# Table scatters of a group made independent, and a second buffer for gathered rows

## The chip, the cores and the metric

The kernel runs on one core of a Trainium2 chip. The metric is device time in microseconds (us) of one execution, taken as the median of three. The engines are named as in the profile: PE (TensorE, matmuls; PEld its weight loads), DVE (VectorE), ACT (ScalarE), POOL (GpSimd) and SP (SyncE, which here only issues DMAs). Each engine runs its own instructions in a fixed order and waits on semaphores for the others and for DMAs.

## The reference

Three layers in a row, in float32. First a chunked attention: 4 batches, 8 heads, 768 positions, chunks of 32 with 16 positions of context to the left, 8 to the right and 8 memory positions. Its output is a matrix of 3072 tokens by 512. Then a dense gated layer, and then a routed layer in which each token goes to one of 8 experts:

```python
g = x @ w_gate;  silu = g * (1.0 / (1.0 + np.exp(-g)));  val = x @ w_val
x = silu * val @ w_out                       # 512 -> 1536 -> 512

logits = x @ w_gate;  e_idx = np.argmax(logits, axis=1)
gate_w = softmax(logits)[np.arange(N), e_idx]
eom = 1.0 / (1.0 + np.exp(-(x @ w_output_gate)))
for e in range(8):
    mask = e_idx == e
    h = np.maximum(x[mask] @ w1[e], 0.0)     # 512 -> 1024
    out[mask] = gate_w[mask, None] * eom[mask, e, None] * (h @ w2[e])
```

## The kernel before

**Groups.** The first two layers run in 8 groups of 384 tokens (`NG`, `GT`). A group's dense layer is 12 chunks `f` of 128 hidden columns: `m1_gate` and `m1_val` (L484, a product of split parts, three matmuls each) and `m1_out` (L525). The weights of each chunk are split anew into a high part, which ACT casts, and a low part, which POOL subtracts (L176, L177: `gvh` and `gvl` for gate and value, `oh` and `ol` for the output). PE needs `gvl` of chunk f + 1 from the third matmul of that chunk on. The attention pieces of the next group are spread between these chunks.

**The table.** When a group is done (`m1_done`), each of its tokens gets an expert and a place in that expert's list. Three scatters (`rt_R`, L668, 128 tokens each, an indirect DMA that POOL issues) write the tokens' numbers into `table` in DRAM, and one DMA of SP writes the tokens' rows into `xs` (L654). `later(delay, ...)` puts such pieces off by a number of ticks; there are three ticks to a chunk `f` in the groups and two to a chunk in the routed layer. The framework makes each scatter wait for the one before it to land, since both write `table`.

**Steps.** The routed layer runs in steps: steps 0, 1 and 2 hold the first 256 tokens of experts 0, 1 and 2 from groups 0 to 6 (`NEARLY` = 3, the early experts), the others are laid out by a schedule that DVE works out from the counts (`make_schedule`). A step has 8 chunks `n` (`NFE`). For a step, SP loads the token numbers out of the table (`load_idx`, tile `idx`, L844), POOL gathers the rows by them (`gather`, tile `xg`, L853, one indirect DMA for 128 rows), `prep_x` transposes them on PE (L871) and splits them. For a chunk, `split_chunk` (L826, L828) makes a high part on ACT and the low part in two halves, one on DVE (for `mm1`) and one on POOL (for `mm2`), under the names `wh`, `wl`, `gvh`, `gvl` in turn. `mm1` (L884) and `mm2` (L906) multiply, and `evac_y` and `scatter_y` (L922, on POOL) send the results out. `mm2` of a chunk stands behind `mm1` of the next.

**The order around the change.** In the last group the `idx` of steps 0 to 2 are loaded at chunk 7, `gather(0)` stands at the end of chunk 8 and `gather(1)` at the end of chunk 11. `xg` has one buffer, so `gather(2)` stands in the first chunk of step 1, behind the transposes of the rows of step 1, and step 2's rows are transposed from the fifth chunk of step 1 on:

```python
if j == 0 and (s >= NEARLY or 0 < s < NEARLY - 1):
    gather(s + 1)
    if s >= NEARLY:
        load_idx(s + 2)
```

The last group's scatters run in step 1 as well; at chunk `ready` = 14 SP loads `idx` of steps 3 and 4, and behind them in SP's queue stand the weight loads of the scheduled steps.

Of the kernel before, what the change touches and what calls it, by code (L numbers as in the profile page):

```python
# [21 lines left out]
def tile_chunk_attention_moe_moe2(  # L22
# [511 lines left out]
    def later(delay, fn, *args):  # L534
        nonlocal serial
        serial += 1
        todo.append((clock + delay, serial, fn, args))
        todo.sort(key=lambda x: x[:2])
# [86 lines left out]
    def rt_2(st, g):  # L625
        ps = ps_a.tile([P, GJ + 1, E], F32, tag="a", name="ps_r")
        for j in range(GJ + 1):
            for i in range(min(j + 1, GJ)):
                nc.tensor.matmul(
                    ps[:, j, :], tri if i == j else ones, st["ohb"][:, i, :],  # L630
                    start=(i == 0), stop=(i == min(j, GJ - 1)))
        r = small("r")
        tt(r, ps[:, 0:GJ, :], base.to_broadcast([P, GJ, E]), ALU.add)
        tt(base, ps[:, GJ:GJ + 1, :], base, ALU.add)
        tt(r, r, st["oh"], ALU.mult)
        pos = small("pos", (P, GJ, 1))
        red(pos, r, ALU.add)
        posi = small("posi", (P, GJ, 1), I32)
        nc.vector.tensor_copy(posi, pos)
        for j in range(GJ):  # L640
            later(1 + (3 if g < NG - 1 else 2) * j, rt_R, posi, g, j)
        if g == NG - 2:
            tt(base, base, mbase, ALU.max)

# [14 lines left out]
    def independent(inst, n, reason):  # L659
# [3 lines left out]
            tc.declare_no_dep(inst.ins, prev.ins, reason=reason)  # L663
        scattered.append(inst)

    def rt_R(posi, g, j):
        tk = g * GJ + j
        nc.gpsimd.indirect_dma_start(  # L668
            out=table, out_offset=bass.IndirectOffsetOnAxis(ap=posi[:, j, :], axis=0),
            in_=tokid[:, tk:tk + 1], in_offset=None)  # L670


    def ts(out_, a, s1, op0, s2=None, op1=None):
# [9 lines left out]
    def make_schedule():  # L683
# [83 lines left out]
        "ra": ("rwa", NRA, [P, 2, KD * P], F32), "w": (wrp, NF, [P, 2, KD * P], F32),  # L767
        "wh": ("p", 2, [P, 2, KD * P], F32R), "wl": ("p", 2, [P, 2, KD * P], F32R),
        "gvh": (jp, 2, [P, 2, KD * P], F32R), "gvl": (jp, 2, [P, 2, KD * P], F32R),
        "idx": (sm, 4, [P, 3], I32), "xg": ("p", 1, [P, 3, XW], F32),  # L770
        "xh": (xp, 2, [P, KD, 2 * P], F32R), "xl": (xp, 2, [P, KD, 2 * P], F32R),
        "sc": (sm, 3, [P, 3, 1], F32), "a": (ps_a, 3, [P, KD, P], F32),
        "g": (ps_g, 2, [P, 2 * P], F32), "o": (ps_o, GJ, [P, DM], F32),
# [58 lines left out]
    def load_idx(s):  # L832
        if s >= NSTEP:
            return
        e, nt = steps[s]
        idx = m2_tile(s, "idx")
        if e is not None:
            src = table[e * ES:e * ES + nt * P, :]
        else:
            d = s - NEARLY  # L840
            rv = nc.sync.value_load(
                sched_i[0:1, 1, d:d + 1], min_val=0, max_val=NTAB - nt * P)
            src = table[bass.ds(rv, nt * P), :]
        nc.sync.dma_start(out=idx[:, 0:nt], in_=src.rearrange("(t p) o -> p (t o)", p=P))  # L844
        idxs[s] = idx

    def gather(s):
# [80 lines left out]
    with tc.manual_schedule():  # L928
# [16 lines left out]
        for g in range(NG):  # L945
# [22 lines left out]
            for f in range(NF):  # L968
# [26 lines left out]
                if g == NG - 1:  # L995
                    if NRA + f < NEARLY * NFE:
                        load_chunk(NRA + f)
                    if f == 7:
                        for s in range(NEARLY):
                            load_idx(s)  # L1000
                    if f == 8:
                        gather(0)
                    if f in (10, 11):
                        prep_x(0, f - 10)
                    if f == 11:
                        gather(1)
                    if f >= 10:
                        split_chunk(f - 10)
        m1_out(NG - 1, NF - 1)
# [17 lines left out]
        def run_step(s, cond):  # L1027
            nonlocal nextc, pend
            for j in range(NFE):
# [19 lines left out]
                pend = (n, h)  # L1049
                if not cond and s + 1 < NUNC and 4 <= j < 7:  # L1050
                    prep_x(s + 1, j - 4)
                if j == 0 and (s >= NEARLY or 0 < s < NEARLY - 1):
                    gather(s + 1)
                    if s >= NEARLY:
                        load_idx(s + 2)
                tick()

        def finish():
# [51 lines left out]
```

## Time and profile before

| | us |
|---|---|
| median of 3 runs | 1177.03 (1175.99 to 1178.24) |
| the profiled execution | 1184.21 |
| span of its instructions | 1182.5 |
| PE busy | 1134.3 (96%) |
| POOL busy | 670.4 (57%) |
| ACT busy | 610.7 (52%) |
| DVE busy | 586.3 (50%) |

A row of a timeline is one instruction, or several alike in a row: start and duration in us, engine, line, operation, the tile written and the tiles read, and in brackets how long the engine had been idle before it and what ended that. The duration of an indirect DMA on POOL is the time in which POOL issues it, not the time until the data have landed. The attention takes the first part of the span, groups 0 to 7 follow one another until about 813 us, and the routed layer ends the program.

### The profile page before, as it was taken

To read this page: it belongs to the slowest core of one execution; us is meant where nothing else is said; L and a number is where in the kernel's file an instruction comes from. 1 tells how busy PE (TensorE), PEld (TensorE's weight loads), DVE (VectorE), ACT (ScalarE), POOL (GpSimd) and SP (SyncE) were. 2 spreads that over 40 slices of the span, in tenths; PEclk is the share of its full clock that TensorE was granted. 3 is DMA by queue.
4 is the path that set the end of the run, shared out by engine and by line. 5 is a ranking of instruction groups with operands and counts; after the bars stand their busy time and mean duration, and the time that the engine had idled before them with its cause. 6 is when DMAs were issued, how large, how long until landed. Compare 5 with 4: busy or idle time off the path is not lost.

```text
span 1182.5 us, 19838 instructions
## 1 busy us (share of the span) xinstructions
PE 1134.3 (96%) x7173; PEld 1019.6 (86%) x7173; DVE 586.3 (50%) x1162; ACT 610.7 (52%) x1318; POOL 670.4 (57%) x459
## 2 busy tenths in 40 slices
PE   7898999999999999999999999989889999999994
PEld 6787899998998998989899899878779899999994
DVE  6699845444444533544543433434854443444541
ACT  4688855555554545555555544434434443344551
POOL 4589844544644654454455465565476555656773
PEclk6799999999999999999999999999989999999998
DMA  8776524111211211211210100344369445555673
GB/s 206 193 216 206 147 78 117 36 35 43 48 30 28 64 35 35 55 43 24 63 37 14 42 7 19 92 96 160 51 186 342 150 146 161 174 162 190 208 221 119
DMA packets 204957, 126.52 MB, mean 107 GB/s; under 512 B 110960, under 2 KB 181744, under 8 KB 204850
## 3 DMA queue, kind: packets, MB, share of 16 engines
q1 hardware_dynamic: 199282, 110.70, 33.5%
q0 software_dynamic: 5568, 14.45, 4.1%
q8 instruction: 59, 0.97, 0.4%
q14 instruction: 48, 0.39, 0.1%
HBM read 111.61 MB, written 14.82 MB: 107 GB/s over the span
## 4 chain that ended last, share of the span: by engine, by line
PE 56%; issue 18%; POOL 8%; DVE 8%; DMA 4%; ACT 4%; SPq 1%; POOLq 0%; ACTq 0%; DVEq 0%
PE ps_g L484 28%; PE acc L525 14%; PE ps_att L350 3%; PE g L884 2%; POOL wl L828 2%; PE ps_pv L402 2%; PE o L906 2%; PE ps_t L322 2%; POOL out_dram L922 2%; POOL gvl L828 1%; PE ps_att L385 1%; PE ps_x L570 1%; DMA xg<-xs,idx 1%; DVE ps_c L225 1%; DVE w L228 1%
## 5 line engine op out<-in xcount | busy, mean ns | idle before, releaser
L177 POOL TENSOR_TENSOR gvl<-w,gvh 128x1024 fp32r<-128x1024 f32 x96 | 231.4, 2411 | 96.2 <-ACT gvh L176 95.3
L484 PE MATMUL ps_g<-xh,gvh 128*128 128x384 f32 x768 | 272.3, 355 | 0.6 <-ACT gvh L176 0.6
L484 PE MATMUL ps_g<-xh,gvl 128*128 128x384 f32 x768 | 262.8, 342 | 6.4 <-POOL gvl L177 6.4
L484 PE MATMUL ps_g<-xl,gvh 128*128 128x384 f32 x768 | 262.4, 342 | 0.0
L177 POOL TENSOR_TENSOR ol<-w,oh 128x512 fp32r<-128x512 f32 x96 | 123.8, 1289 | 187.2 <-ACT oh L176 185.1
L525 PE MATMUL acc<-oh,h 128*128 128x512 f32 x576 | 202.0, 405 | 0.0
L484 PEld LDWEIGHTS ps_g<-xh,gvl 128*128 128x128 f32 x768 | 146.0, 190 | 8.4 <-POOL gvl L177 8.4
L497 DVE SCALAR_TENSOR_TENSOR th<-th,ps_g 128x384 f32<-128x384 f32 x96 | 53.1, 553 | 198.6 <-ACT th L492 198.6
L484 PEld LDWEIGHTS ps_g<-xh,gvh 128*128 128x128 f32 x768 | 146.2, 190 | 4.0 <-issue 0.7
L484 PEld LDWEIGHTS ps_g<-xl,gvh 128*128 128x128 f32 x768 | 146.3, 190 | 1.9
L525 PEld LDWEIGHTS acc<-oh,h 128*128 128x128 f32 x576 | 108.2, 188 | 23.4 <-issue 1.4
L508 ACT CAST h<-th 128x384 fp32r<-128x384 f32 x96 | 49.3, 513 | 145.7 <-DVE th L506 144.7
L888 ACT ACTIVATE h<-g 128x256 fp32r<-128x256 f32 (+1 forms) x96 | 41.1, 429 | 160.9 <-PE g L884 158.3
L525 PE MATMUL acc<-ol,h 128*128 128x512 f32 x288 | 113.7, 395 | 0.3 <-POOL ol L177 0.3
L890 DVE SCALAR_TENSOR_TENSOR h<-g,h 128x256 fp32r<-128x256 f32 (+1 forms) x96 | 45.8, 477 | 119.6 <-ACT h L888 119.6
L176 ACT CAST gvh<-w 128x1024 fp32r<-128x1024 f32 x96 | 100.1, 1044 | 0.2
L492 ACT ACTIVATE th<-ps_g 128x384 f32<-128x384 f32 x96 | 46.9, 488 | 94.9 <-PE ps_g L484 94.7
L514 DVE TENSOR_TENSOR h<-th,h 128x384 fp32r<-128x384 f32 x96 | 71.9, 749 | 30.5 <-ACT h L508 30.5
L506 DVE TENSOR_TENSOR th<-th,ps_g 128x384 f32<-128x384 f32 x96 | 53.0, 552 | 68.4 <-PE ps_g L484 68.2
L906 PE MATMUL o<-gvh,h 128*128 128x512 f32 x232 | 80.7, 396 | 1.6 <-DVE h L890 1.6
L906 PE MATMUL o<-wh,h 128*128 128x512 f32 x232 | 81.4, 399 | 0.0
L828 POOL TENSOR_TENSOR wl<-w,wh 128x512 fp32r<-128x512 f32 x30 | 50.5, 1685 | 38.6 <-ACT wh L826 36.0
(192 smaller groups left out, 2411.3 us busy)
## 6 DMA issues: line engine op xcount, KB each, us to landing
w<-in_moe_w_dram SPq DMA_DIRECT2D x120, 256.0 KB
ra<-in_moe_w_dram SPq DMA_DIRECT2D x72, 256.0 KB
kt<-in_k_dram SPq DMA_DIRECT2D x35, 176.0 KB
vt<-in_v_dram SPq DMA_DIRECT2D x35, 176.0 KB
xs<-xr SPq DMA_DIRECT2D x8, 769.5 KB
st<-in_moe_w_gate_dram SPq DMA_DIRECT2D x12, 512.0 KB
st<-in_moe_w_val_dram SPq DMA_DIRECT2D x12, 512.0 KB
st<-in_moe_w_out_dram SPq DMA_DIRECT2D x12, 512.0 KB
```

Of the source, the lines that this page charges most:

```text
L176: nc.scalar.copy(out=hi, in_=src)
L177: lo_eng.tensor_tensor(out=lo, in0=src, in1=hi.bitcast(F32), op=ALU.subtract)
L484: nc.tensor.matmul(ps, a[:, c], x[:, kk, :], start=(n == 0), stop=(n == 3 * KD - 1))
L492: nc.scalar.activation(out=th, in_=ps, func=AF.Tanh, scale=0.5)
L497: nc.vector.scalar_tensor_tensor(out=th, in0=th, scalar=1.0, in1=ps, op0=ALU.add, op1=ALU.mult)
L506: nc.vector.tensor_tensor(out=hh, in0=hh, in1=ps, op=ALU.mult)
L508: nc.scalar.copy(out=h1, in_=hh)
L514: nc.vector.tensor_tensor(out=h2, in0=hh, in1=h1.bitcast(F32), op=ALU.subtract)
L525: nc.tensor.matmul(accs[g][j], a[:, c], w_, start=(f == 0 and n == 0), stop=(f == NF - 1 and n == 2))
L828: eng.tensor_tensor(out=b[:, i], in0=r[:, i], in1=a[:, i].bitcast(F32), op=ALU.subtract)
L890: nc.vector.scalar_tensor_tensor(out=h2, in0=ps, scalar=0.0, in1=h1.bitcast(F32), op0=ALU.max, op1=ALU.subtract)
L906: nc.tensor.matmul(ysd[s][t], hx[:, c], wx[:, 1], start=(j == 0 and i == 0), stop=(j == NFE - 1 and i == 2))
```

## The change

- The three scatters of a group no longer depend on one another. The first scatter of the next group waits for all three of the last one. All three go out two ticks apart in every group; before, three ticks apart except in the last group.
- SP's loads of `idx` wait for all three scatters of the last group that was listed; before, for the last scatter, which waited for the others.
- `xg` has two buffers.
- `gather(1)` stands at the end of chunk 9 of the last group, and `gather(2)` in the first chunk of step 0, two steps ahead. From step 3 on the gathers stand where they stood.

```diff
-            later(1 + (3 if g < NG - 1 else 2) * j, rt_R, posi, g, j)
+            later(1 + 2 * j, rt_R, posi, g, j)
...
+    listed = []
+
+    def after(inst, prev, reason):
+        tc.add_manual_dep(
+            inst.ins, prev.ins.name,
+            mybir.DependencyInfo(mybir.DependencyClass.Sync, mybir.DependencyReason.DATA),
+            reason=reason)
+
     def rt_R(posi, g, j):
         tk = g * GJ + j
-        nc.gpsimd.indirect_dma_start(
+        inst = nc.gpsimd.indirect_dma_start(
             out=table, out_offset=bass.IndirectOffsetOnAxis(ap=posi[:, j, :], axis=0),
             in_=tokid[:, tk:tk + 1], in_offset=None)
+        if j == 0:
+            for prev in listed:
+                after(inst, prev, "the next group's entries follow the last group's")
+            listed.clear()
+        for prev in listed:
+            tc.declare_no_dep(inst.ins, prev.ins, reason="the tokens of a group have their own entries")
+        listed.append(inst)
...
-        "idx": (sm, 4, [P, 3], I32), "xg": ("p", 1, [P, 3, XW], F32),
+        "idx": (sm, 4, [P, 3], I32), "xg": ("p", 2, [P, 3, XW], F32),
...
-        nc.sync.dma_start(out=idx[:, 0:nt], in_=src.rearrange("(t p) o -> p (t o)", p=P))
+        inst = nc.sync.dma_start(out=idx[:, 0:nt], in_=src.rearrange("(t p) o -> p (t o)", p=P))
+        for prev in listed:
+            after(inst, prev, "all entries of the table are there")
...
                     if f == 8:
                         gather(0)
+                    if f == 9:
+                        gather(1)
                     if f in (10, 11):
                         prep_x(0, f - 10)
-                    if f == 11:
-                        gather(1)
...
-                if j == 0 and (s >= NEARLY or 0 < s < NEARLY - 1):
+                if j == 0 and s < NEARLY - 2:
+                    gather(s + 2)
+                if j == 0 and s >= NEARLY:
                     gather(s + 1)
-                    if s >= NEARLY:
-                        load_idx(s + 2)
+                    load_idx(s + 2)
```

The order of PE, DVE, ACT and SP is the same as before; POOL's is not. The first place is POOL in the last group of the dense layer, from the instruction behind group 6's first scatter on. Before:

```order
L177 TENSOR_TENSOR gvl<-w,gvh 128x1024
L177 TENSOR_TENSOR ol<-w,oh 128x512
L668 DMA table<-tokid,posi 28672x1
L177 TENSOR_TENSOR gvl<-w,gvh 128x1024
L177 TENSOR_TENSOR ol<-w,oh 128x512
L668 DMA table<-tokid,posi 28672x1
L177 TENSOR_TENSOR gvl<-w,gvh 128x1024
L177 TENSOR_TENSOR ol<-w,oh 128x512
L853 DMA xg<-xs,idx 128x513 x2
L177 TENSOR_TENSOR gvl<-w,gvh 128x1024
```

The same place in the changed kernel, whose lines have moved (L676 is the scatter, L870 the gather):

```order
L177 TENSOR_TENSOR gvl<-w,gvh 128x1024
L676 DMA table<-tokid,posi 28672x1
L177 TENSOR_TENSOR ol<-w,oh 128x512
L676 DMA table<-tokid,posi 28672x1
L177 TENSOR_TENSOR gvl<-w,gvh 128x1024
L177 TENSOR_TENSOR ol<-w,oh 128x512
L177 TENSOR_TENSOR gvl<-w,gvh 128x1024
L177 TENSOR_TENSOR ol<-w,oh 128x512
L870 DMA xg<-xs,idx 128x513 x2
L177 TENSOR_TENSOR gvl<-w,gvh 128x1024
L177 TENSOR_TENSOR ol<-w,oh 128x512
L870 DMA xg<-xs,idx 128x513 x2
```

The second and third scatter have moved ahead by one and three operations of L177, and `gather(1)`, the last row, stands one chunk behind `gather(0)`.

The second place is POOL in step 1, from the last group's first scatter on, with the semaphores that each row waits for (DMASW is an indirect DMA's, DMAHW one of SP's, the others an engine's). Before:

```order
L668 DMA table<-tokid,posi 28672x1 [waits DMAHW6_49,DMASW4_49,DVE_49]
L828 TENSOR_TENSOR gvl<-w,gvh 128x512 [waits PE_49,Activation_49]
L668 DMA table<-tokid,posi 28672x1 [waits DMASW1_49]
L853 DMA xg<-xs,idx 128x513 [waits DMAHW3_49,DMASW7_49,DMASW0_49]
L853 DMA xg<-xs,idx 128x513
L828 TENSOR_TENSOR gvl<-w,gvh 128x512 [waits DMAHW7_49,PE_49,Activation_49]
L668 DMA table<-tokid,posi 28672x1 [waits DMASW2_49]
L922 DMA out_dram<-yo,idx 3072x512
L828 TENSOR_TENSOR wl<-w,wh 128x512 [waits DMAHW1_49,PE_49,Activation_49]
```

The same place in the changed kernel (L843 is the split, L939 the scatter of results):

```order
L676 DMA table<-tokid,posi 28672x1 [waits DMASW4_49,DMASW3_49,DVE_49]
L843 TENSOR_TENSOR gvl<-w,gvh 128x512 [waits PE_49,Activation_49]
L676 DMA table<-tokid,posi 28672x1
L843 TENSOR_TENSOR gvl<-w,gvh 128x512 [waits DMAHW7_49,PE_49,Activation_49]
L676 DMA table<-tokid,posi 28672x1
L939 DMA out_dram<-yo,idx 3072x512
L843 TENSOR_TENSOR wl<-w,wh 128x512 [waits DMAHW1_49,PE_49,Activation_49]
```

The two gathers of step 2 have gone from here, and the second and third scatter wait for nothing.

## Rows read from the trace of the kernel before

**Rows 1.** The page: the busy time of PE.

```profile
PE 1134.3 (96%) x7173; PEld 1019.6 (86%) x7173; DVE 586.3 (50%) x1162; ACT 610.7 (52%) x1318; POOL 670.4 (57%) x459
```

**Rows 2.** The timeline of PE, waits and the work behind them.

```profile
514.99 0.44 PE L484 MATMUL ps_g<-xh,gvl 128*128 128x384 f32 x1 [1.43 <-POOL gvl L177]
...
786.61 0.44 PE L484 MATMUL ps_g<-xh,gvl 128*128 128x384 f32 x1 [1.60 <-POOL gvl L177]
...
795.73 0.69 PE L484 MATMUL ps_g<-xh,gvl 128*128 128x384 f32 x1 [2.54 <-POOL gvl L177]
...
799.09 0.34 PE L484 MATMUL ps_g<-xh,gvh 128*128 128x384 f32 x1
799.27 0.34 PE L484 MATMUL ps_g<-xl,gvh 128*128 128x384 f32 x1
...
801.04 0.33 PE L484 MATMUL ps_g<-xh,gvl 128*128 128x384 f32 x1
...
862.27 1.08 PE L871 MATMUL a<-ident,xg 128*128 128x128 f32 x4 [5.74 <-DMA xg<-xs,idx]
...
867.87 0.60 PE L871 MATMUL a<-ident,xg 128*128 128x128 f32 x4
...
871.15 0.28 PE L884 MATMUL g<-xh,gvh 128*128 128x256 f32 x1
```

**Rows 3.** Busy time by stretch; behind the engines the granted clock, DMA share, GB/s.

```profile
796.00:799.00 3.00, 3.00 (x10) 3.00 (x11) 0.00 (x0) 0.00 (x0) 3.00 (x2) 0.50 0.24 72
```

**Rows 4.** The timeline of POOL in group 4, in group 7 and in step 1.

```profile
511.24 1.30 POOL L668 DMA_INDIRECT table<-tokid,posi  x1 [4.69 <-DMA table<-tokid,posi]
...
767.14 0.99 POOL L668 DMA_INDIRECT table<-tokid,posi  x1 [0.15 <-issue]
...
773.85 0.98 POOL L668 DMA_INDIRECT table<-tokid,posi  x1 [0.89 <-DMA table<-tokid,posi]
...
783.18 0.98 POOL L668 DMA_INDIRECT table<-tokid,posi  x1 [3.90 <-DMA table<-tokid,posi]
...
786.50 1.28 POOL L177 TENSOR_TENSOR ol<-w,oh 128x512 fp32r<-128x512 f32 x1
790.79 0.99 POOL L853 DMA_INDIRECT xg<-xs,idx  x1 [3.01 <-DMA idx<-table]
...
793.33 2.35 POOL L177 TENSOR_TENSOR gvl<-w,gvh 128x1024 fp32r<-128x1024 f32 x1
...
842.02 1.00 POOL L668 DMA_INDIRECT table<-tokid,posi  x1 [1.10 <-DVE xi L681]
843.04 1.30 POOL L828 TENSOR_TENSOR gvl<-w,gvh 128x512 fp32r<-128x512 f32 x1
850.18 1.00 POOL L668 DMA_INDIRECT table<-tokid,posi  x1 [5.83 <-DMA table<-tokid,posi]
...
859.03 1.00 POOL L668 DMA_INDIRECT table<-tokid,posi  x1 [3.98 <-DMA table<-tokid,posi]
...
861.34 1.31 POOL L828 TENSOR_TENSOR wl<-w,wh 128x512 fp32r<-128x512 f32 x1
```

**Rows 5.** The tiles `table` and `xg`: from issue to landing of their DMAs.

```profile
DMA to landing us min/median/max: 4.2/8.0/10.2
...
DMA to landing us min/median/max: 3.8/4.6/13.2
```

**Rows 6.** The timeline of SP: loads of `idx`.

```profile
787.69 1.39 SPq L844 DMA_DIRECT2D idx<-table  x3
...
868.66 1.64 SPq L844 DMA_DIRECT2D idx<-table  x2
```

**Rows 7.** The timeline of DVE in step 1: two halves of the split.

```profile
842.51 2.39 DVE L828 TENSOR_TENSOR wl<-w,wh 128x512 fp32r<-128x512 f32 x1
...
850.63 0.69 DVE L828 TENSOR_TENSOR wl<-w,wh 128x512 fp32r<-128x512 f32 x1 [0.28 <-ACT wh L826]
```

**Rows 8.** The timeline of ACT in step 1: a cast.

```profile
846.73 1.04 ACT L826 CAST gvh<-w 128x1024 fp32r<-128x1024 f32 x1
```

## The prediction

> **What bounds the kernel now.** I read the page's engine line first: TensorE (PE) is busy 96% of the span [rows 1]. A change that takes no matmul away can win only where PE stands idle or runs slow, so the next view was PE's timeline, filtered to rows with a wait behind them. Three places matter [rows 2]: at 514.99 us PE waits 1.43 us for a `gvl` of GpSimd (POOL); at 786.61 and 795.73, in the last group of the first expert layer, 1.60 and 2.54 us for the next two `gvl`; at 862.27, in step 1 of the routed layer, 5.74 us for gathered rows `xg`. Behind the last two PE also runs slow: the granted clock is 0.50 in 796 to 799, the lower of its two levels [rows 3]. Ten matmuls take 795.73 to 799.09 = 3.36 us there, and ten take 799.27 to 801.04 = 1.77 us afterwards: 1.59 us lost. One transpose block, one `mm1` and one `mm2` take 862.27 to 867.87 = 5.60 us, and the same work 867.87 to 871.15 = 3.28 us: 2.32 us lost [rows 2].
>
> Then I asked what POOL did ahead of each place [rows 4]. At 511.24 the third table scatter of a group starts after 4.69 us of waiting for the scatter before it, and the `gvl` for 514.99 stands behind it. In group 6 the second and third scatters wait 0.89 and 3.90 us, the third goes out at 783.18, and POOL then waits 3.01 us for `idx` until 790.79, because SP's loads of `idx` had to wait for that third scatter until 787.69 [rows 6]; only after two gathers does the `gvl` start at 793.33. In group 7 the waits are 5.83 and 3.98 us, up to 850.18 and 859.03, and the two gathers of step 2 sit between those scatters. A scatter lands a median of 8.0 us after its issue (4.2 to 10.2), a gather 4.6 us, but one of them 13.2 us [rows 5]: the gathers queued behind the second scatter are the ones that hold PE until 862.27.
>
> **The change, part by part.** No instruction is added on PE, DVE or ACT, and their order stays the same; only POOL's order moves, and a few waits.
>
> (a) Scatters of groups 0 to 5. The second and third of each group lose their wait and go out two ticks apart. POOL's stalls disappear; PE pays for one of them that I count, 1.43 us at 514.99 [rows 2]. The scatter that now stands right behind a `gvl` delays the `ol` behind it by its own 0.98 us [rows 4]; `ol` is used a whole chunk later, so I cost that at nothing; if that cover were gone it would be about 1 us in a chunk, with six groups that have such a place. Gain 1.43 us.
>
> (b) Scatters of group 6, `idx` and the first gathers. Without the waits POOL issues the scatters at 767.14, then behind a `gvl` (2.35 us) at 770.5, and behind an `ol` (1.28 us) at 772.8 [rows 4]. The `gvl` needed at 786.61 then loses the 3.90 us in front of it, and its 1.60 us on PE go. SP's `idx` loads now wait for all three scatters. If the landings overlap, the last is there by 772.8 + 10.2 = 783.0 us even at the slowest landing [rows 5]. From SP's issue to the gather it took 790.79 - 787.69 = 3.10 us [rows 4, 6], so rows can be asked for from 786.1. Before, POOL was ready for them at 786.50 + 1.28 = 787.78, so the 3.01 us wait is gone. Next late: gathers and gaps take 793.33 - 790.79 = 2.54 us, the `gvl` 2.35 us, so it ends by 786.1 + 4.9 = 791.0. PE wants it at 795.73 - 2.54 - 1.60 = 791.6. The margin is 0.6 us, thin but there. So 2.54 us and the 1.59 us at half clock go too: 1.60 + 2.54 + 1.59 = 5.73 us. If the landings do not overlap, the scatters land as before at 773.85, 783.18 and 787.69, the gather waits as before, and (b) is worth nothing, since what PE saves at 786.61 it waits longer for at 795.73. I take 5.73 and keep 0 as the other end.
>
> (c) `gather(1)` moves from the end of chunk 11 to that of chunk 9: 2 issues, 2.54 us of POOL with gaps, one chunk behind `gather(0)`. POOL's load in such a chunk is one `gvl` (2.35), one `ol` (1.28) and this, 6.2 us; from 786.61 less its 1.60 us wait to 795.73 less 2.54 and 1.60 PE asks for a `gvl` every 6.6 us. It fits; if it does not, the price is under 1 us. No gain, no cost. Where it stood, POOL is free earlier for `wl`, which nothing waits for.
>
> (d) Step 2's rows two steps ahead, into a second buffer. `gather(2)` is issued in the first chunk of step 0, and PE wants it at 862.27 - 5.74 = 856.5, in the fifth chunk of step 1: 12 chunks later, which at some 3 us each (3.28 with a transpose block) is over 30 us. Against that stand 2.54 us to issue and 13.2 us to land at worst [rows 4, 5]; the cover is over 15 us. The write of `xs` for the last group on SP now also waits for this gather, which has landed before. PE's 5.74 us and the 2.32 us at half clock go: 8.06 us.
>
> (e) Scatters of group 7. What would be late next is in [rows 4]: the `wl` half at 861.34 ends at 862.65, because the third scatter held POOL until 859.03, and with the rows there PE would want it at about 858.4 (856.5 and just over half of the 3.28 us, for `mm2` comes last in them). So (d) alone would be stopped after 2 us. With (e) POOL runs `gvl` to 844.34 and the second scatter at once; the next `gvl` can start when ACT's cast ends, 846.73 + 1.04 = 847.8 [rows 8], the third scatter and one scatter of results follow at 849.1 and 850.1, and this `wl` ends by 852.4. Both parts are needed for the 8.06 us. SP's next `idx` loads were issued at 868.66 [rows 6]; now they wait for the three scatters, 850, 858 and 866 us if they land one after another, which is no later than before.
>
> (f) A cost the trace does not show: POOL's second scatter of group 7 now follows a `gvl` without a gap. A `wl` half on DVE took 2.39 us at 842.51 beside a scatter and that `gvl`, and 0.69 us at 850.63 beside a scatter alone [rows 7]. Bounds: 0 (the second row) and 2.39 - 0.69 = 1.70 us (the first). I take 0.5, nearer the row with the scatter alone.
>
> Sum on the profiled execution: 1.43 + 5.73 + 8.06 - 0.5 = 14.7 us, from 1184.2 to 1169.5. The median of the timed runs is 7.2 us below the profiled execution. If all of that excess lay in the DMA waits above, only 7.5 us would be saved there; if none, 14.7. I take off 1.7, as the excess more likely lies over the whole span: 13.0 us, 1177.0 - 13.0 = **1164.0 us**.
>
> **A rule against (b).** The row: one gather behind a scatter landed after 13.2 us in place of 4.6 [rows 5], as if the queue let nothing pass until the scatter's entries were written. By that the scatters land one after another and the sum is 9.0. The Trainium skill, "DMA: Bandwidth & Descriptors", section "Queues, rings and completion order", says that data descriptors carry no barrier and that only the semaphore's increment is ordered behind the earlier writes of its engine. By that rule the landings overlap and the sum is 14.7; the trace does not settle it, as no two scatters are in flight together in it.
>
> **Rivals.**
> One after another: the scatters land as in (b)'s other end. For it: the 13.2 us. Against it: a landing of 8 us for 128 entries of 4 bytes looks like latency, not like work in the queue. 1.43 + 8.06 - 0.5 = 9.0 us, less 0.8 of the excess: 1168.8 us.
> The wait only changes its name: PE reaches 858.4 and POOL still holds the `wl` half until 862.65, since the scatters still wait on POOL. Then 8.06 less 4.25 and less some 2.3 at half clock: 1.5 us are left, 1175.5. Against it: in the new order the second and third scatters carry no wait at all.
> Slower, one mechanism: POOL and DVE shut each other out. Each scatter that now stands without a gap between two POOL operations makes one DVE operation up to 1.70 us longer [rows 7]; there are 24 scatters, and it decides from the ninth that PE has to wait for (14.7 / 1.70 = 8.6). With 12 of them, 20.4 us, and 13.0 gained: 1184.4 us. Against it: scatters stood right in front of a `gvl` before as well, and in the groups PE is held by POOL in [rows 2], never by DVE. The Trainium skill, "SBUF — State Buffer", section "SBUF: two separate sides", has the two engines take a shared pair of ports as an exclusive lock for a whole instruction. By that rule the price would be one POOL instruction each time; the row at 842.51 agrees with it, the row at 850.63 does not.
>
> **How the numbers follow.** Forecast 0.60, with a range of its own of 1161.8 (15.2 us, no cost in (f)) to 1167; one after another 0.24; the changed name 0.10; slower 0.06. No change means within 0.2%, 2.4 us, about what a measurement of this kernel can tell. Faster: 0.60 + 0.24 + half of the third, 0.89. Same: the other half and 0.01 of the last, 0.06. Slower: 0.05. The range takes in the first two cases: from 1161.8 less the 1.1 us by which the runs lie apart, 1160.7, up to 1170.5, where one after another meets the 7.2 us of excess in part.
>
> **What the changed profile would show.** (a), (b): no row of a scatter with a wait for a scatter, and no PE wait at the places of 514.99 and 786.61. (b): SP's three `idx` loads issued by 783 rather than 787.69 and the gather behind them without idle time; if they are still issued past 786, the scatters land one after another. (d), (e): no wait for `xg`, no half clock in step 1, the `wl` half done 4 us before its `mm2`. Wrong would be: a PE wait on a POOL `gvl` behind the two early gathers, DVE halves of 2 us and more with PE waiting for them, or a time above 1171.

## The result, and the profile after

| | before | changed |
|---|---|---|
| median of 6 runs, us | 1178.66 (1175.99 to 1181.30) | 1167.07 (1166.19 to 1168.53) |
| the profiled execution, us | 1184.21 | 1166.49 |
| its span, us | 1182.5 | 1164.8 |

The changed kernel takes 0.9903 of the time of before (95% interval 0.9886 to 0.9921), 11.6 us less. The forecast was 1164.0 us with a range of 1160.7 to 1170.5; the time lies in the range, 3.1 us above the forecast.

The page of the changed kernel shows the work unchanged; for the same 7173 instructions PE is busy 7.8 us less than in [rows 1], since less of it runs at the lower clock (the mean granted clock of the span is 0.982, before 0.975).

```profile
PE 1126.5 (97%) x7173; PEld 1013.2 (87%) x7173; DVE 588.9 (51%) x1162; ACT 611.1 (52%) x1318; POOL 670.3 (58%) x459
```

POOL's timeline of the changed kernel, at the places of [rows 4] (a scatter is L676 now, a gather L870, the split L843, the scatter of results L939):

```profile
489.76 1.13 POOL L676 DMA_INDIRECT table<-tokid,posi  x1 [0.16 <-issue]
...
584.99 1.12 POOL L676 DMA_INDIRECT table<-tokid,posi  x1 [0.16 <-issue]
...
762.14 0.99 POOL L676 DMA_INDIRECT table<-tokid,posi  x1 [0.15 <-issue]
...
765.73 0.98 POOL L676 DMA_INDIRECT table<-tokid,posi  x1 [0.17 <-issue]
...
768.22 0.98 POOL L676 DMA_INDIRECT table<-tokid,posi  x1 [0.17 <-issue]
...
782.92 0.99 POOL L870 DMA_INDIRECT xg<-xs,idx  x1 [2.30 <-DMA w<-in_moe_w_dram]
784.21 0.95 POOL L870 DMA_INDIRECT xg<-xs,idx  x1 [0.30 <-PE ps_g L484]
785.18 2.38 POOL L177 TENSOR_TENSOR gvl<-w,gvh 128x1024 fp32r<-128x1024 f32 x1
...
832.30 1.00 POOL L676 DMA_INDIRECT table<-tokid,posi  x1 [1.10 <-DVE xi L696]
...
834.79 1.26 POOL L676 DMA_INDIRECT table<-tokid,posi  x1 [0.17 <-issue]
...
840.12 1.07 POOL L676 DMA_INDIRECT table<-tokid,posi  x1 [0.16 <-issue]
...
843.13 1.34 POOL L843 TENSOR_TENSOR wl<-w,wh 128x512 fp32r<-128x512 f32 x1
844.64 1.01 POOL L939 DMA_INDIRECT out_dram<-yo,idx  x1 [0.17 <-DVE pk L594]
845.65 1.32 POOL L843 TENSOR_TENSOR wl<-w,wh 128x512 fp32r<-128x512 f32 x1
846.91 1.28 POOL L843 TENSOR_TENSOR gvl<-w,gvh 128x512 fp32r<-128x512 f32 x1
```

No second or third scatter waits for a scatter any more. But POOL still stands idle for 2.30 us ahead of the first gather, and the `gvl` behind the two gathers ends at 787.56. PE's timeline of the changed kernel, all waits of group 6 to step 1 for POOL, DVE or a DMA, with step 2's first two transpose blocks and the first `mm2` matmul that takes POOL's `wl` half:

```profile
787.62 0.44 PE L484 MATMUL ps_g<-xh,gvl 128*128 128x384 f32 x1 [1.28 <-POOL gvl L177]
...
801.60 0.50 PE L525 MATMUL acc<-ol,h 128*128 128x512 f32 x1 [0.31 <-POOL ol L177]
...
832.92 0.73 PE L923 MATMUL o<-gvh,h 128*128 128x512 f32 x2 [1.64 <-DVE h L907]
...
835.24 0.38 PE L901 MATMUL g<-xh,wl 128*128 128x256 f32 x1 [0.90 <-DVE wl L843]
...
846.42 0.60 PE L888 MATMUL a<-ident,xg 128*128 128x128 f32 x4
...
848.80 0.39 PE L901 MATMUL g<-xh,wl 128*128 128x256 f32 x1 [1.54 <-DVE wl L843]
...
850.29 0.39 PE L923 MATMUL o<-wl,h 128*128 128x512 f32 x1
...
851.44 0.60 PE L888 MATMUL a<-ident,xg 128*128 128x128 f32 x4
```

Against [rows 2]: the waits of 1.43, 1.60 and 5.74 us are gone, the 2.54 us for the `gvl` behind the first two gathers have become 1.28 us, and a wait of 1.54 us for DVE is new; those of 1.64 and 0.90 us for DVE stood in the kernel before as well. Behind none of them does PE slow down: the granted clock is 1.00 in 787 to 792, in 832 to 840 and in the stretch of step 1 shown here (busy time by stretch of the changed kernel; the last three figures of a row are the granted clock, the DMA share and GB/s), where it was 0.50 behind one of the old waits [rows 3].

```profile
840.00:860.00 20.00, 18.46 (x119) 16.30 (x118) 16.24 (x38) 9.53 (x15) 12.78 (x10) 1.00 0.25 76
```

The ledger comes from POOL's first scatter of a group as a marker. Two markers of the kernel before, from POOL's timeline, complete [rows 4]:

```profile
490.96 1.13 POOL L668 DMA_INDIRECT table<-tokid,posi  x1 [0.16 <-issue]
...
590.01 1.11 POOL L668 DMA_INDIRECT table<-tokid,posi  x1 [0.16 <-issue]
```

| stretch, profiled executions | before | changed | gain |
|---|---|---|---|
| start to the scatter at 490.96 / 489.76 | 490.96 | 489.76 | 1.20 |
| to the scatter at 590.01 / 584.99 (group 3's scatters, sent in group 4) | 99.05 | 95.23 | 3.82 |
| to 767.14 / 762.14 | 177.13 | 177.15 | -0.02 |
| to 842.02 / 832.30 (group 6's scatters, first gathers) | 74.88 | 70.16 | 4.72 |
| to the end of the span (step 1 and all behind it) | 340.48 | 332.50 | 7.98 |

The sum is 17.7 us, 6.1 us more than the medians show: the profiled execution of before was a long one (above all six runs in the table; of that kernel's 43 runs beside the experiments two took longer, up to 1184.71 us), that of the changed kernel was not. Two parts of the sum lie where the change does nothing that the prediction names. The 1.20 us of the first row are there by the program's first scatter (205.02 before, 203.83 changed), ahead of all that was edited. Of the last row, 1.27 us lie behind step 2's second transpose block (867.87 before, 851.44 changed): up to that block the gain is (867.87 - 842.02) - (851.44 - 832.30) = 6.71 us.

### The profile page after: what moved, and what is told of

The parts are those of the page before. It is cut to its first block, busy times and chain, and to the rows that moved or that the text cites. A ratio compares the mean times of both kernels' runs of the same rounds, so it can differ in the third digit from the quotient of the medians.

```text
span 1164.8 us, 19839 instructions
## 1 busy us (share of the span) xinstructions
PE 1126.5 (97%) x7173; PEld 1013.2 (87%) x7173; DVE 588.9 (51%) x1162; ACT 611.1 (52%) x1318; POOL 670.3 (58%) x459
## 4 chain that ended last, share of the span: by engine, by line
PE 78%; DVE 9%; ACT 4%; issue 3%; POOL 3%; DMA 2%; SPq 0%; POOLq 0%; ACTq 0%; DVEq 0%
PE ps_g L484 30%; PE acc L525 15%; PE g L901 11%; PE o L923 11%; PE ps_att L350 3%; PE ps_pv L402 2%; PE ps_t L322 2%; PE ps_att L385 2%; PE ps_x L570 1%; DVE ps_c L225 1%; DVE w L228 1%; ACT s L364 1%; DVE ps_c L223 1%; PE a L888 1%; ACT qbd L309 1%
## 5 line engine op out<-in xcount | busy, mean ns | idle before, releaser
L177 POOL TENSOR_TENSOR gvl<-w,gvh 128x1024 fp32r<-128x1024 f32 x96 | 231.5, 2412 | 109.7 <-ACT gvh L176 107.0
L177 POOL TENSOR_TENSOR ol<-w,oh 128x512 fp32r<-128x512 f32 x96 | 123.8, 1289 | 195.9 <-ACT oh L176 193.7
L843 POOL TENSOR_TENSOR wl<-w,wh 128x512 fp32r<-128x512 f32 x30 | 50.5, 1686 | 37.6 <-ACT wh L841 34.6
```

Source lines behind the costliest of these rows:

```text
L177: lo_eng.tensor_tensor(out=lo, in0=src, in1=hi.bitcast(F32), op=ALU.subtract)
L843: eng.tensor_tensor(out=b[:, i], in0=r[:, i], in1=a[:, i].bitcast(F32), op=ALU.subtract)
```

## The experiments

Each group of runs had its own runs of the kernel before, with medians of 1180.84 (the first four), 1181.11 (the next four) and 1179.42 us (the last two). What a kernel gained is worked out below as one less the ratio, times that median.

| kernel | median us | ratio to before (95%) |
|---|---|---|
| independent scatters, old gathers | 1172.41 | 0.9928 (0.9913 to 0.9942) |
| early gathers, old scatters | 1177.09 | 0.9979 (0.9967 to 0.9991) |
| the change, scatters three ticks apart | 1173.73 | 0.9941 (0.9928 to 0.9954) |
| independent scatters in groups 0 to 5 only | 1178.82 | 0.9982 (0.9973 to 0.9991) |
| the changed kernel again | 1168.33 | 0.9893 (0.9872 to 0.9914) |
| first gathers behind the split | 1165.93 | 0.9865 (0.9845 to 0.9884) |
| results of step 0 later | 1167.81 | 0.9884 (0.9866 to 0.9903) |
| three edits together | 1163.34 | 0.9837 (0.9818 to 0.9857) |
| last group's gate values later | 1167.34 | 0.9898 (0.9878 to 0.9918) |
| gathers and last group's gate values | 1164.42 | 0.9872 (0.9851 to 0.9892) |

### Only the scatters

The edit takes the second buffer and the new places of the gathers back out of the changed kernel:

```diff
-        "idx": (sm, 4, [P, 3], I32), "xg": ("p", 2, [P, 3, XW], F32),
+        "idx": (sm, 4, [P, 3], I32), "xg": ("p", 1, [P, 3, XW], F32),
...
-                    if f == 9:
-                        gather(1)
                     if f in (10, 11):
                         prep_x(0, f - 10)
+                    if f == 11:
+                        gather(1)
...
-                if j == 0 and s < NEARLY - 2:
-                    gather(s + 2)
-                if j == 0 and s >= NEARLY:
+                if j == 0 and (s >= NEARLY or 0 < s < NEARLY - 1):
                     gather(s + 1)
-                    load_idx(s + 2)
+                    if s >= NEARLY:
+                        load_idx(s + 2)
```

> Only the scatters' half of the change: the three scatters of a group independent and two ticks apart, idx loads behind all three; one buffer for xg, gather(1) at the end of chunk 11 and gather(2) in step 1 as before. Theory 1 (PE was held by POOL's stalls behind scatters in the groups, and in step 1 by late rows and by the wl half together): the groups' part is kept whole (PE waits on gvl in the last group 1.3 us in place of 4.1, none in group 4), and in step 1 gather(2) goes out behind the second scatter at about 837 us, lands 7 to 10 us later, so PE waits 0 to 3 us for xg instead of 5.7; in all 8 to 11 us faster than before (ratio 0.990 to 0.993). Theory 2 (the early gathers and the second buffer make the whole gain): within 2 us of before. Theory 3 (the scatters make the whole gain): the whole 11.6 us.

It gained 0.0072 x 1180.84 = 8.5 us. PE's timeline shows what the gathers would have had to remove, the wait for rows in step 1, and ahead of it the wait in the last group:

```profile
789.54 0.44 PE L484 MATMUL ps_g<-xh,gvl 128*128 128x384 f32 x1 [3.07 <-POOL gvl L177]
...
851.00 0.63 PE L888 MATMUL a<-ident,xg 128*128 128x128 f32 x4 [2.42 <-DMA xg<-xs,idx]
```

So independent scatters alone shorten the wait for `xg` from 5.74 to 2.42 us: gathers that no scatter holds up go out earlier (840.81 in place of 851.48), though the two still take 10.1 and 12.1 us to land. The wait of 3.07 us is a miss: 1.3 us were expected, as in the changed kernel, whose POOL order this is up to the first gather. From SP's `idx` loads to that gather it took 784.88 - 779.87 = 5.01 us here; more on this step below.

### Only the gathers

The kernel before with the gathers and the second buffer of the change, and its scatters chained as they were:

```diff
-        "idx": (sm, 4, [P, 3], I32), "xg": ("p", 1, [P, 3, XW], F32),
+        "idx": (sm, 4, [P, 3], I32), "xg": ("p", 2, [P, 3, XW], F32),
...
+                    if f == 9:
+                        gather(1)
...
-                    if f == 11:
-                        gather(1)
...
-                if j == 0 and (s >= NEARLY or 0 < s < NEARLY - 1):
+                if j == 0 and s < NEARLY - 2:
+                    gather(s + 2)
+                if j == 0 and s >= NEARLY:
                     gather(s + 1)
-                    if s >= NEARLY:
-                        load_idx(s + 2)
+                    load_idx(s + 2)
```

> Only the gathers' half of the change: two buffers for xg, gather(1) at the end of chunk 9, gather(2) in step 0; the scatters wait for each other as before, with the old ticks. Theory 1: no wait for xg any more, but PE then waits some 4 us in step 1 for the wl half that POOL reaches only after the third scatter, and runs at half clock behind it; waits on gvl in group 4 and in the last group stay. 1 to 3 us faster than before. Theory 2: 11.6 us faster. Theory 3: no change.

It gained 2.5 us. PE's timeline of this kernel has no wait for `xg`, but this one:

```profile
858.02 0.80 PE L906 MATMUL o<-wl,h 128*128 128x512 f32 x1 [4.06 <-POOL wl L828]
```

and POOL's timeline says why:

```profile
853.93 0.98 POOL L668 DMA_INDIRECT table<-tokid,posi  x1 [6.62 <-DMA table<-tokid,posi]
855.22 1.45 POOL L922 DMA_INDIRECT out_dram<-yo,idx  x1 [0.30 <-issue]
856.65 1.31 POOL L828 TENSOR_TENSOR wl<-w,wh 128x512 fp32r<-128x512 f32 x1
```

The third scatter waits for the second, and the `wl` half stands behind it. This is the rival in which the wait only changes its name; its 4.25 us came out as 4.06, and the granted clock behind it is 0.50 (857 to 863). In the change it does not happen, because there the scatters wait for nothing.

The two runs add up: 8.5 + 2.5 = 11.0 us, against 11.4 and 12.6 us for the whole change in its two timings. By their intervals the halves are worth 6.8 to 10.3 and 1.1 to 3.9 us, so a part that only both together bring could hide in this sum.

### Scatters three ticks apart

```diff
-            later(1 + 2 * j, rt_R, posi, g, j)
+            later(1 + (3 if g < NG - 1 else 2) * j, rt_R, posi, g, j)
```

> The changed kernel with the old spacing: scatters of groups 0 to 6 independent but three ticks apart. Theory 1: group 6's third scatter goes out two ticks, some 4 to 6 us, later, idx lands later by about that less the overlap of the landings, the first gather and the gvl behind it with it; PE waits 4 to 6 us on gvl there in place of 1.3, partly at half clock behind it, so 3 to 6 us slower than the changed kernel (6 to 9 us faster than before). Rival (spacing plays no part, only the waits do): as the changed kernel, 11.6 us faster.

It gained 7.0 us, where the changed kernel gained 11.4 and 12.6. POOL's timeline has the third scatter of group 6 go out 12.27 us behind the first (6.08 in the changed kernel), and the gather waits for it:

```profile
763.98 0.98 POOL L676 DMA_INDIRECT table<-tokid,posi  x1 [0.16 <-issue]
...
776.25 0.98 POOL L676 DMA_INDIRECT table<-tokid,posi  x1 [0.15 <-issue]
...
787.93 0.99 POOL L870 DMA_INDIRECT xg<-xs,idx  x1 [5.51 <-DMA idx<-table]
```

PE then waits 4.45 us for the `gvl` behind it, as its timeline shows:

```profile
792.60 0.45 PE L484 MATMUL ps_g<-xh,gvl 128*128 128x384 f32 x1 [4.45 <-POOL gvl L177]
```

From the first scatter of group 6 to that of group 7 this execution needs 838.81 - 763.98 = 74.83 us, against 74.88 before and 70.16 in the changed kernel. Independence without the closer places bought nothing in group 6.

### Independent scatters in groups 0 to 5 only

Groups 6 and 7 chained at the old places, old gathers, one buffer. Against the kernel before, cut to what the changed kernel does not have:

```diff
-            later(1 + (3 if g < NG - 1 else 2) * j, rt_R, posi, g, j)
+            later(1 + (2 if g == NG - 1 or g < NG - 2 else 3) * j, rt_R, posi, g, j)
...
+        for prev in listed:
+            if g < NG - 2:
+                tc.declare_no_dep(inst.ins, prev.ins, reason="the tokens of a group have their own entries")
+            else:
+                after(inst, prev, "one after another")
```

> Only the scatters of groups 0 to 5 independent and two ticks apart; those of groups 6 and 7 wait for each other with the old ticks, gathers and buffer as before. Theory 1: only part (a) is left, PE's waits for gvl in group 4 and the half clock behind them, 1.4 to 3.8 us by the profiles; in the timed runs 0 to 4 us faster than before. Theory 2: no change. Theory 3: half of 11.6 us or more, if the stalls of every group counted.

It gained 2.1 us (1.1 to 3.2 by the interval). Its profiled execution needs 585.37 - 490.15 = 95.22 us from the scatter of group 3 to that of group 4, as the changed kernel does, and has no wait for POOL in group 4. So these scatters are what took 3.82 us out of that stretch. That the timed gain is smaller is seen in the trace of the kernel with only the gathers, whose scatters here are those of before (POOL's timeline):

```profile
490.58 1.12 POOL L668 DMA_INDIRECT table<-tokid,posi  x1 [0.16 <-issue]
...
586.76 1.12 POOL L668 DMA_INDIRECT table<-tokid,posi  x1 [0.15 <-issue]
```

The same work took 96.18 us there, 0.95 more than in the changed kernel and not 3.82. What the chained scatters cost in a group differs from one execution to the next. Group 6 shows the same: chained at the old places, it needs 835.42 - 762.53 = 72.89 us in the kernel with groups 0 to 5 free, to the first scatter of group 7, and 74.88 in the kernel before.

### The changed kernel again, and three edits of it

Two waits are left that one can aim at: 1.28 us at 787.62 and 1.54 us at 848.80. The first edit calls the first two gathers right behind the split of `gv` rather than ahead of the next one:

```diff
                     split_gv((f + 1) % NF)
+                if g == NG - 1 and f in (9, 10):
+                    gather(f - 9)
...
-                    if f == 8:
-                        gather(0)
-                    if f == 9:
-                        gather(1)
```

the second puts the scatters of step 0's results off, and the third the piece `rt_3` of the last group (the third was run in the kernel with all three first). `rt_3` does no table scatter: DVE works out the group's gate values in it (`se`, `xr`), and SP writes `xs`. The last two expectations below call it the table scatters; those are `rt_R`, which this edit does not touch:

```diff
-            later(1 + 2 * t, scatter_y, yo, idx, t)
+            later((6 if s == 0 else 1) + 2 * t, scatter_y, yo, idx, t)
```

```diff
-        later(12, rt_3, st, g)
+        later(12 if g < NG - 1 else 16, rt_3, st, g)
```

> The changed kernel again, beside the three below on the same chip. Theory 1: the parts add up: groups 0 to 5 alone gave 2.0 us, gathers alone 2.5 us, scatters alone 8.5 us, and the whole is more than the 11.0 us of the two halves only by what each half kept from the other in step 1 (2.4 us of waiting for rows in the one, 4.1 us for the wl half in the other): 10 to 13 us faster than before.

> The changed kernel with gather(0) and gather(1) each moved behind the next chunk's gvl on POOL, which stood behind them. Theory 1 (the 1.28 us on PE that are left in the last group come from POOL standing at gather(0) for idx, 2.3 us, in front of the gvl): that wait goes, the rows still land before their transposes two chunks later; 1 to 2 us faster than the changed kernel. Rival (the gvl is late because POOL has too much to do in these chunks): the wait only moves to the next gvl or ol; no change.

> The changed kernel with the two scatters of step 0's results five ticks later, so that they no longer stand between the wl halves of step 1. Theory 1 (the new wait of 1.54 us for a DVE wl half comes from POOL and DVE shutting each other out, as the scatters of the table and of the results push POOL's halves together): the 3.5 us DVE half falls to 2 us or less and PE's wait with it; 1 to 1.5 us faster than the changed kernel. Rival (DVE is late by its own work on the schedule): the wait stays, no change.

> Both of the edits above, and the last group's row of gate values (se, xr and the write of xs) four ticks later, so that DVE reaches the last group's table positions and the h of step 1 sooner. Theory 1: the waits of 1.28 and 1.54 us and part of the 1.6 + 0.9 us for DVE's h and wl at the last group's first scatter go; 2 to 5 us faster than the changed kernel. Rival (PE's waits at that point are DVE's total work, which stays): 2 us or less.

The changed kernel came out at 1168.33 us, with the same five waits in its trace to 0.04 us. With the gathers behind the split it was 1165.93, and the wait at 787.62 is gone; the intervals of the two ratios overlap. The 1.54 us are gone from that trace too, though the edit did not aim at them: the DVE half there took 2.29 us, and PE waits 0.53 us for `h` in its place. With the results later it was 1167.81, no difference that can be told. Yet what it aimed at is gone: the DVE half that had taken 3.50 us takes 0.67 us, as DVE's timeline shows, first of the changed kernel and then of the one with the results later:

```profile
845.25 3.50 DVE L843 TENSOR_TENSOR wl<-w,wh 128x512 fp32r<-128x512 f32 x1
```

```profile
847.06 0.67 DVE L843 TENSOR_TENSOR wl<-w,wh 128x512 fp32r<-128x512 f32 x1
```

In the same trace PE's timeline shows where the profiled execution lost it again: its wait for the first `gvl` behind the gathers was longer, in code that this edit does not touch, and PE came out of it at the lower clock (0.50 in 788 to 791). Whether the timed runs lost it there is not shown.

```profile
787.83 0.69 PE L484 MATMUL ps_g<-xh,gvl 128*128 128x384 f32 x1 [2.06 <-POOL gvl L177]
788.32 0.52 PE L484 MATMUL ps_g<-xh,gvh 128*128 128x384 f32 x1
```

All three edits together took 1163.34 us, 5.0 us under the median of the changed kernel beside it, with intervals that do not touch: this version beats both kernels. Its granted clock is 1.00 from 780 to 860.

### Which of the three

> The changed kernel with one edit: the table scatters of the last group alone (the piece rt_3, which also starts the counts for the schedule) come four ticks, two chunks, later in the routed layer. Of the 5 us by which the kernel with three edits beat the changed one, two places in its trace can be the source: in the last group the 1.3 us wait for gvl and what is slow behind it (gathers moved behind the split of gv), and in step 1 the stretch 828 to 860 (this edit, or the later results). Theory: this edit spreads the short DVE work of the schedule away from the halves of wl, so that no half on DVE is held for over 2 us; PE's wait of 1.54 us for the 3.50 us half goes, and the time is about 2.5 us under the changed kernel's 1168.3, so 1165.8, ratio 0.987. Rival 1: only the later results free DVE, this edit alone leaves the 1.54 us wait, and the time is the changed kernel's, ratio 0.989 to 0.990. Rival 2: the third scatter comes so late that the idx loads of steps 3 and 4 are behind it; then the next scheduled steps wait and it is slower than the changed kernel.

> Two of the three edits together: gather(0) and gather(1) behind the split of gv of chunks 9 and 10, and the last group's table scatters four ticks later; the scatters of results stay where the change has them. Theory: the two edits act at different places (before 800 us and after 828 us), so their gains add: about 2 us from the gathers (1.3 us of wait and part of the slow matmuls behind it) and 2.5 us from the later scatters, about 1163.8 and a ratio of 0.985, within a microsecond of the kernel with all three (1163.3, 0.984). Rival: the third edit, results later, carries step 1; then this is no better than the gathers alone, 1165.9, ratio 0.9865.

What the third edit moves is SP's write of `xs`, from 831.25 in the changed kernel to 836.86 here, and DVE's four operations ahead of it; the table scatters start at 832.17, where they started at 832.30. Alone it took 1167.34 us: its ratio of 0.9898 is the changed kernel's. The theory's step in the trace came true (no DVE half above 0.67 us until 851, the 1.54 us wait gone), but not the gain; in its place PE waits three times for DVE's `h`, 0.84 + 0.66 + 1.23 = 2.73 us, where the changed kernel's waits in this stretch were 1.64 + 0.90 + 1.54 = 4.08, so that 1.35 us at most were to be had in it. The wait of 1.23 us stands behind a small DVE operation of the schedule that took 2.20 us here and 0.30 us in the changed kernel (DVE's timeline):

```profile
840.06 2.20 DVE L594 TENSOR_TENSOR ge<-pcum,pk 1x152 f32<-1x152 f32 x1
```

POOL issued a scatter of results from 839.56 to 840.76 and worked on a `wl` half behind it without a gap, until 842.09. So DVE was held here too, and only at another instruction. With the gathers the time was 1164.42 us, a ratio of 0.9872. That is no better than the gathers alone (0.9865), as the rival has it, and its interval also meets that of all three (0.9837). That the gathers belong to the gain is seen in the trace: the wait behind them is gone. Of the results edit the traces show a part: PE's third wait for `h` is 1.20 us without it and 0.35 us with all three. In the timed runs, how the rest divides between the other two edits stays open, as these ratios do not separate them.

## Why the prediction came out right, and where it did not

**(a), groups 0 to 5, 1.43 us: mis-sized.** The wait at 514.99 is gone, but the stretch gained 3.82 us in the profiled executions. I had counted the wait and not looked at the rows behind it. Busy time by stretch of the kernel before:

```profile
515.80:517.80 2.00, 2.00 (x8) 2.00 (x8) 0.00 (x0) 0.00 (x0) 2.00 (x2) 0.50 0.08 18
```

Its PE ran at the lower clock there until about 519.2, the same thing that I had priced at the two other waits and left out here. The matmuls from 515.45 to 519.57 took 4.12 us, the same ones in the changed kernel (511.98 to 514.54) 2.56: that is 1.56 of the 2.39 us. In the timed runs the term is worth 2.1 us, nearer to mine, because the profiled execution was an unlucky one in this group.

**(b), group 6, 5.73 us: right in kind, 4.72 us in size; 1.28 us were left.** Counted from the first scatter, the third was expected 5.7 us later and came 6.08 us later; it landed after 10.2 us, just the bound that I had taken. SP's `idx` loads were expected by 783.0 - 767.14 = 15.9 us and came after 16.42 us. SP's timeline of the changed kernel:

```profile
778.56 1.39 SPq L859 DMA_DIRECT2D idx<-table  x3
```

The step that failed is the next one: from SP's issue to the gather I took the 3.10 us of before, and it was 782.92 - 778.56 = 4.36 us. Late by 1.26 us here and by 0.5 us before, less the margin of 0.6 us that I called thin, makes 1.2 us, and PE waits 1.28. POOL's row names a weight load (`w`) as the last that this gather waited for, and in the kernel with three ticks, where it names `idx`, the step took 787.93 - 784.83 = 3.10 us again. So it goes in the others: 3.10 or 3.11 us in the four kernels whose `idx` loads went out over 7 us behind the weight loads before them, 4.0 to 5.3 us in the seven where it was 3.7 to 5.0 us and POOL waited. That the weight loads delay `idx` is my reading of these rows; no run took them away.

Two signs that I had set down for being wrong are in the trace, then, with the time in its range: a PE wait on the `gvl` behind the two early gathers (1.28 us), and a long DVE half with PE waiting for it ((f), 1.54 us). Nor is 4.72 us sure: from the first scatter of group 6 to that of group 7 it took 70.21 us in the changed kernel's second profiled execution and 72.43 us in the kernel with the results later, whose edit comes behind it, and 72.89 with chained scatters in another kernel. By these executions (b) is worth anything from 0.5 to 4.7 us.

**The rule on landings.** Neither landings as short as before, all at once, nor the rival's queue is what the trace shows. In the changed kernel the DMA issues of group 6 give 6.5, 7.1 and 10.2 us to landing: issues at 762.14, 765.73 and 768.22 land at 768.6, 772.8 and 778.4, so 3.6 and 2.5 us apart on issue become 4.2 and 5.6 us apart on landing. In group 0 the three took 10.8, 13.0 and 15.9 us. The tile `table` as a whole, against [rows 5]:

```profile
DMA to landing us min/median/max: 4.4/9.9/15.9
```

So scatters in flight together land later, by what is not shown, but the three together need some 16 us in group 6, where the chained ones needed 787.69 - 767.14 = 20.6 us. By the Trainium skill, "DMA: Bandwidth & Descriptors", section "Queues, rings and completion order", data descriptors carry no barrier (it says so of the DMAs of SP and ACT; the scatters are POOL's); the trace agrees as far as the second scatter lands less than a landing's length behind the first, and it shows that this does not make each landing as short as a lone one.

**(c), gather(1) two chunks earlier, nothing:** no wait stands behind it in the changed kernel's trace.

**(d) and (e), step 1, 8.06 us: right.** From the first scatter of group 7 to step 2's second transpose block the profiled execution gained 6.71 us, which is 8.06 less the 1.54 us of (f) and 0.2 us more. That the ledger's 7.98 us is so near to 8.06 is chance: 1.27 us of it come later. Rows are there before PE wants them (846.42, 851.44), the gathers' landings have a maximum of 7.6 us in place of 13.2, and the `wl` half that POOL starts at 843.13 is done at 844.47, 5.8 us before PE takes it at 850.29. Step 1 began 9.72 us earlier than before, so this is 854.2 on the old scale, where I had 852.4: late by 1.8 us, and still in time. That both parts are needed is shown: 2.42 us of wait for rows without (d), 4.06 us for `wl` without (e).

**(f), POOL and DVE shutting each other out, 0.5 us: mis-sized, 1.54 us, and at another place.** The half of 2.39 us [rows 7] was there before and is there after, with its 0.90 us of PE. New is the half at 845.25: it ends at 848.75, 0.56 us behind the last of the POOL operations that follow one another without a gap from 844.64 to 848.19, and PE waits 1.54 us. It is one such wait of PE and not nine or more, and the time fell, so the slower rival is refuted. By the Trainium skill, "SBUF — State Buffer", section "SBUF: two separate sides", the two engines exclude each other for a whole instruction, and the one that starts first has the ports. This half agrees in that it ended only when POOL's run had; but it was held over two POOL operations (845.65 to 848.19) and not one, and by the recorded starts it began 0.40 us ahead of the first. In the kernel with the results later, the half at 847.06 began just behind the start of a scatter's issue (846.94 to 848.63 on POOL) and took 0.67 us: there the issue did not hold DVE. Where POOL went on without a gap, it was otherwise: in the changed kernel a small DVE operation began within a scatter's issue (842.52; POOL's scatter until 843.14) and took 1.99 us, until POOL's `wl` half behind the scatter had ended at 844.47. What tells these cases apart no run varied.

**The size of the whole.** The terms came to 14.7 us where the profiles gained 17.7: short by 2.4 in (a), by the 1.2 ahead of the first marker and the 1.27 behind step 1, too large by 1.0 in (b) and by 0.85 in step 1, where (f) was 1.54 and not 0.5. From them I took 1.7 of the 7.2 us by which the profiled execution lay above the median. Between profiles and medians it was 17.7 - 11.6 = 6.1 us. So two errors met, terms too small by 3.0 and a deduction too small by 4.4, and the gain came out 1.4 us below the 13.0 forecast; that they met so closely is luck. The other 1.6 us of the 3.1 are the median of before, which more runs put at 1178.66 instead of 1177.03. That group 4 cost 0.95 us in one execution and 3.82 in another, with the same scatters, shows some of the excess in the waits for DMAs, where I had put little of it.

## What to carry to other kernels

Where a wait is taken away, price the rows behind it as well as the wait: read the granted clock there, every time. Where a chain of DMAs loses its waits, look for what is next on the same engine before believing the gain, since the earlier rows alone were worth 2.5 us and together with free scatters the whole of 11.6. A term that rests on waits for DMAs in one execution is worth that execution's figure only there; a second execution of the same code puts a size on its spread.

## What was not expected of the hardware

The clock behind a wait is not told by the wait's length. PE's wait of 0.90 us for a DVE half left the clock at 1.00 in the changed kernel, and at 0.50, the lower level, for at least three microseconds in the kernel with the gathers behind the split. Its PE timeline and busy time by stretch:

```profile
834.98 0.58 PE L901 MATMUL g<-xh,wl 128*128 128x256 f32 x1 [0.90 <-DVE wl L843]
```

```profile
835.00:836.00 1.00, 1.00 (x5) 1.00 (x5) 0.90 (x5) 0.00 (x0) 0.80 (x1) 0.50 0.00 0
836.00:837.00 1.00, 1.00 (x6) 1.00 (x6) 0.93 (x6) 0.00 (x0) 0.00 (x0) 0.50 0.02 1
837.00:838.00 1.00, 1.00 (x5) 0.90 (x4) 0.61 (x4) 0.48 (x2) 0.00 (x0) 0.50 0.00 0
```

A longer wait, 1.54 us at 848.80 in the changed kernel, left the clock at 1.00, and so did 3.07 us at 789.54 in the kernel with only the scatters (1.00 in 789 to 793); behind the same 2.54 us in the last group the clock was 0.50 before [rows 3] and 1.00 in the kernel with groups 0 to 5 free (790 to 794). What tells them apart these rows do not show, and no run varied it. So a price for half clock behind a wait, as I put it in (b), is itself a draw. And the scatters of group 6, which had needed 6.4, 9.1 and 4.5 us in the kernel before, one in flight at a time, needed 6.5, 7.1 and 10.2 us when they were in flight together, for 128 entries of 4 bytes each.
